# One load for wq, and K and V exchanging their regions of the on-chip buffer, in a decode attention kernel

## The chip, the cores and the metric

The kernel runs on one core of one Trainium2 chip. The metric is device time in microseconds (us) of one execution; lower is better. The engines named below are PE (matrix products), DVE (vector), ACT (scalar) and SP, which does no arithmetic here and only issues the loads. Each core has 16 DMA engines; a load over 128 partitions is cut into packets that all 16 engines carry.

Differences are taken only between kernels of the same batch on the same chip.

## The reference, cut to what matters

One token goes through a gated mix of two branches. Branch A is attention with 32 query heads over 4 groups of cached keys and values; branch B is a small gated MLP.

```python
q = x @ wq                          # wq: 1024 x 4096, bf16, 8.4 MB
scores = q . k_cache * Dh ** -0.5   # k_cache: 4 groups x 65536 x 128, 67 MB
o = softmax(scores) . v_cache       # v_cache: the same size
a = o @ wo                          # 8.4 MB
b = mlp(x, w_in, w_out)             # 7.3 MB and 3.7 MB
out = g * a + (1 - g) * b           # g = sigmoid(sum(x * gate_w))
```

Everything is read once: 162.0 MB for a result of 1024 numbers.

## The kernel before: the parts that matter

One tile `kv` holds all big operands. It has five regions of 32 KB per partition. `load(src, shape, at)` issues a load from SP into the region `at`, and the scheduler adds the waits for whatever still uses those bytes. Issues stay in program order, so one that waits holds up all issues after it.

```python
NKV = 5
kv = big.tile([P, NKV * CT * P], BF16, name="kv")
def load(src, shape, at): ...                       # nc.sync.dma_start(...)
def load_kv(src, g, j, at, n=1): ...                # n tiles of 32 KB per partition
...
win = load(win_view, (KC, F), 3)                    # 56 KB per partition: regions 3 and 4
wq_t = [load(wq_view[:, i * KH:(i + 1) * KH, :], (KH, HD), 1 - i) for i in range(2)]
...                                                 # z from win, q from wq, weights from q
build_w(0)
for j in range(NT):                                 # first group: four K tiles
    k_tile(0, j, load_kv(A_k_cache, 0, j, (2, 1, 0, 3)[j])[0])
    if j == 1:
        build_w(1)
project(load(B_w_out..., (FC, D), 4), ...)
stats(0)
for g in range(1, G):
    for h in range(2):
        kn = load_kv(A_k_cache, g, 2 * h, 1 - h, 2) # K pair: regions 1,2 then 0,1
        for i in ((0, 1), (1, 0))[h]:
            k_tile(g, 2 * h + i, kn[i])
        ...
        vn = load_kv(A_v_cache, g - 1, 2 * h, 3, 2) # V pair: always regions 3,4
        v_tile(g - 1, 2 * h, vn[0])
        if h == 1:
            stats(g)
        v_tile(g - 1, 2 * h + 1, vn[1])
    head_out(g - 1)
```

A K tile is transposed in place on DVE in four pieces; PE multiplies each. The two K pairs of a group overlap by one region, and the order of the tiles is chosen so that the shared region comes free first.

Of the kernel before, what the change touches and what calls it, by code (L numbers as in the profile page):

```python
# [24 lines left out]
WO_SPLIT = ((16,), (8, 4, 2, 1, 1))  # L25
# [4 lines left out]
def kernel(  # L30
# [19 lines left out]
    HD = A_wq.shape[1]  # L50
# [4 lines left out]
    KC = D // P  # L55
# [3 lines left out]
    NT = S // (P * CT)  # L59
# [20 lines left out]
    def same_weights(ins):  # L80
        held.add(ins.ins.name)
# [79 lines left out]
    def load(src, shape, at):  # L161
        n = 1
        for s in shape:
            n *= s
        v = kv[:, int(at * CT * P):int(at * CT * P) + n]
        if len(shape) == 2:
            v = v.rearrange("p (a b) -> p a b", b=shape[1])
        ins = nc.sync.dma_start(out=v, in_=src)  # L168
        if not first_load:
            first_load.append(ins.ins.name)  # L170
        return v

    def load_kv(src, g, j, at, n=1):
        h, i = divmod(j, 2)
        rows = src[0, g, 2 * h * CT * P:2 * (h + 1) * CT * P, :].rearrange(
            "(p c) d -> p (c d)", c=2 * CT)
        v = load(rows[:, i * CT * DH:(i + n) * CT * DH], (n * CT * DH,), at)
        return [v[:, i * CT * DH:(i + 1) * CT * DH] for i in range(n)]
# [9 lines left out]
    KH = KC // 2  # L188
# [1 line left out]
    win = load(win_view, (KC, F), 3)  # L190
    win_t = [win[:, i * KH:(i + 1) * KH, :] for i in range(2)]
    wq_view = A_wq.rearrange("(p c) n -> p c n", c=KC)
    wq_t = [load(wq_view[:, i * KH:(i + 1) * KH, :], (KH, HD), 1 - i) for i in range(2)]


    row = const.tile([P, P], FP32, name="row")
# [147 lines left out]
    for k in range(NHB):  # L344
# [3 lines left out]
                                                                   j=B, e=2),  # L348
# [20 lines left out]
    def build_w(g):  # L369
        for v in range(VC):  # L370
            nc.vector.tensor_tensor(
                out=wt[g % 2][:, v, :, :, v, :],
                in0=qs[:, g].unsqueeze(2).to_broadcast([P, BP, NB, REP]),
                in1=own_n[:].unsqueeze(1).unsqueeze(3).to_broadcast([P, BP, NB, REP]),
                op=ALU.mult)
# [5 lines left out]
    def k_tile(g, j, kn):  # L381
        kb = kn.bitcast(I32)
        n = CC * DH // 2
        s_ps = pss.tile([P, 2 * HN], FP32, name="s_ps", tag="s")
        for v in range(VC):
            nc.vector.transpose(out=kb[:, v * n:(v + 1) * n], in_=kb[:, v * n:(v + 1) * n])  # L386
            while late:
                nc.vector.reduce_max(**late.pop())  # L388
            kx = kn[:, v * CC * DH:(v + 1) * CC * DH].rearrange(
                "p (c h k e) -> p h e c k", h=2, k=B, e=2)  # L390
            for b in range(BP):
                for k in range(2):
                    ins = nc.tensor.matmul(  # L393
                        s_ps[:, k * HN:(k + 1) * HN],
                        lhsT=wt[g % 2][:, v, b].rearrange("p a v h -> p (a v h)"),
                        rhs=kx[:, b // 2, b % 2, k * CC // 2:(k + 1) * CC // 2, :],
                        start=(v == 0 and b == 0), stop=(v == VC - 1 and b == BP - 1),
                        skip_group_check=True)
                    if k > 0:
                        same_weights(ins)  # L400
        if g not in mxs:
            mxs[g] = wk.tile([P, NT], FP32, name="mx")
        sct[g, j] = scp.tile([P, CC * B], BF16, name="sc")
        nc.scalar.copy(out=sct[g, j][:], in_=s_ps[:])  # L404
        late.append(dict(out=mxs[g][:, j:j + 1], in_=sct[g, j][:], axis=AX.X))

    def stats(g):
        nc.vector.reduce_max(**late.pop())  # L408
        m1 = wk.tile([P, 1], FP32, name="m1")
        nc.vector.reduce_max(out=m1[:], in_=mxs[g][:], axis=AX.X)  # L410
        mt_ps = psm.tile([1, P], FP32, name="mt_ps", tag="m")
        nc.tensor.transpose(mt_ps[:], m1[:], ident_f[:])
        gm = wk.tile([1, REP], FP32, name="gm")
        nc.vector.tensor_reduce(out=gm[:], in_=mt_ps[:].rearrange("p (a h) -> p h a", h=REP),
                                axis=AX.X, op=ALU.max)
        gr = wk.tile([1, P // REP, REP], FP32, name="gr")
        nc.vector.tensor_copy(out=gr[:], in_=gm[:].unsqueeze(1).to_broadcast([1, P // REP, REP]))
        nb_ps = psm.tile([P, 1], FP32, name="nb_ps", tag="m")
        nc.tensor.matmul(nb_ps[:], lhsT=gr[:].rearrange("p a h -> p (a h)"),
                         rhs=ones_f[0:1, 0:1], start=True, stop=True)  # L420
        nb = wk.tile([P, 1], FP32, name="nb")
        nc.vector.tensor_scalar(out=nb[:], in0=nb_ps[:], scalar1=-SCALE, scalar2=None,  # L422
                                op0=ALU.mult)
        lss[g] = wk.tile([P, NT], FP32, name="ls")
        for j in range(NT):
            nc.scalar.activation(out=sct[g, j][:], in_=sct[g, j][:], func=ACT.Exp, scale=SCALE,  # L426
                                 bias=nb[:, 0:1], accum_out=lss[g][:, j:j + 1])
            ptt[g, j] = ptp.tile([P, CC, B], BF16, name="pt")
            nc.vector.transpose(out=ptt[g, j][:].rearrange("p c x -> p (c x)"),  # L429
                                in_=sct[g, j][:])  # L430

    def v_tile(g, j, vt):
        if j == 0:
            o_ps[g] = pso.tile([P, 2, VC * DH], FP32, name="o_ps")
        vx = vt.rearrange("p (v c d) -> p c v d", v=VC, d=DH)
        for u in range(CC // 2):
            hs = slice(u % 2 * P // 2, (u % 2 + 1) * P // 2)
            for e in range(2):
                ins = nc.tensor.matmul(  # L439
                    o_ps[g][hs, e, :],  # L440
                    lhsT=ptt[g, j][:, 2 * u:2 * u + 2, :].rearrange("p c x -> p (c x)"),
                    rhs=vx[:, 2 * u + e], start=(j == 0 and u < 2),
                    stop=(j == NT - 1 and u >= CC // 2 - 2), skip_group_check=True)
                if e > 0:
                    same_weights(ins)
# [28 lines left out]
    def keep_busy(n):  # L474
        ps = pss.tile([P, 2 * HN], FP32, name="busy_ps", tag="s")
        w = wt[G % 2][:].rearrange("p v b t u h -> p (v b t u h)")
        for i in range(n):
            ins = nc.tensor.matmul(ps[:, :HN], lhsT=w[:, :P], rhs=w[:, :HN], start=True,  # L478
                                   stop=True, skip_group_check=True)
            if i > 0:  # L480
                same_weights(ins)
# [4 lines left out]
    def project(w, n, vec, c0, first=False, last=False):  # L486
        for c in range(n):
            for t in range(NB):
                nc.tensor.matmul(  # L489
                    out_ps[t * B:(t + 1) * B, :],  # L490
                    lhsT=vec[:, c0 + c:c0 + c + 1].to_broadcast([P, B]),
                    rhs=w[:, c, t * NO:(t + 1) * NO],
                    start=(first and c == 0), stop=(last and c == n - 1),
                    skip_group_check=True)


    build_w(0)
    for j in range(NT):
        k_tile(0, j, load_kv(A_k_cache, 0, j, (2, 1, 0, 3)[j])[0])
        if j == 1:  # L500
            build_w(1)
    project(load(B_w_out.rearrange("(p c) n -> p c n", c=FC), (FC, D), 4), FC, uT, 0, first=True)
    stats(0)
    for g in range(1, G):
        for h in range(2):
            kn = load_kv(A_k_cache, g, 2 * h, 1 - h, 2)
            for i in ((0, 1), (1, 0))[h]:
                k_tile(g, 2 * h + i, kn[i])
            if h == 0 and g + 1 < G:
                build_w(g + 1)  # L510
            vn = load_kv(A_v_cache, g - 1, 2 * h, 3, 2)
            v_tile(g - 1, 2 * h, vn[0])
            if h == 1:
                stats(g)
            v_tile(g - 1, 2 * h + 1, vn[1])
        head_out(g - 1)
    for j, n, at in ((0, 2, 1), (2, 1, 3), (3, 1, 4)):
        for i, vt in enumerate(load_kv(A_v_cache, G - 1, j, at, n)):
            v_tile(G - 1, j + i, vt)
    keep_busy(4)  # L520
# [3 lines left out]

    wo_view = A_wo.rearrange("(p c) n -> p c n", c=OC)
    c0 = 0
    for at, split in enumerate(WO_SPLIT):
        for n in split:
            t = load(wo_view[:, c0:c0 + n, :], (n, D), at + c0 % (OC // 2) * D / (CT * P))
            project(t, n, oa, c0, last=(c0 + n == OC))  # L530
            keep_busy(WO_BUSY[n])
            c0 += n
# [46 lines left out]
```

## Time and profile before

| | before |
|---|---|
| time, median (5 runs) | 383.12 us |
| span of the profiled run | 381.3 us |
| PE, DVE busy | 61%, 57% |
| load queue, share of the time of 16 DMA engines | 98.7% |
| 65,536-byte packet on one engine (median) | 2.421 us |
| last load complete | 378.36 us |

From the page of the kernel before: the span, the busy shares of the engines, the mean DMA share in 40 slices of the span (9 is 90% or more), and the load queue with its packets, megabytes and share of 16 engines' time.

```profile
span 381.3 us, 2601 instructions
PE 233.9 (61%) x1388; PEld 56.2 (15%) x802; DVE 218.5 (57%) x211; ACT 39.6 (10%) x55; POOL 4.4 (1%) x10
...
DMA  9999999999999999999999999999999999999995
...
DMA packets 4231, 162.17 MB, mean 425 GB/s; under 512 B 504, under 2 KB 508, under 8 KB 892
...
q1 hardware_dynamic: 4180, 162.01, 98.7%
```

The loads fill the time; every slice but the last is at 9. A packet of 65,536 bytes in 2.421 us is 27.1 GB/s on one engine and 433 GB/s on 16. The Trainium skill, "DMA: Bandwidth & Descriptors", Specifications, gives 435 GB/s as the fabric ceiling, and this trace agrees within 0.5%. So the DMA engines are not only busy, they are at their rate.

Part 4 of the same page follows the work that ended last back through what released it.

```profile
DMA 58%; PE 25%; DVE 13%; ACT 2%; issue 1%; SPq 1%; DVEq 0%; ACTq 0%
```

Read alone, this chain says that 38% of the time belongs to PE and DVE. It does so because each load was *issued* after some matmul or transpose freed its region. That does not tell whether the issue came late. For this one needs the queue's own times (columns: start, length, operation, count; several issues are merged, so a length covers the waits between them). Kernel before, issues from SP:

```profile
0.79 0.80 SPq L168 DMA_DIRECT2D kv<-in_A_wq_dram  x2
1.64 42.21 SPq L168 DMA_DIRECT2D kv<-in_A_k_cache_dram  x4
43.90 0.92 SPq L168 DMA_DIRECT2D kv<-in_B_w_out_dram  x1
73.52 0.33 SPq L168 DMA_DIRECT2D kv<-in_A_k_cache_dram  x1
96.88 0.33 SPq L168 DMA_DIRECT2D kv<-in_A_v_cache_dram  x1
119.44 0.33 SPq L168 DMA_DIRECT2D kv<-in_A_k_cache_dram  x1
```

The trace also records every packet. Each engine closes a load with a 4-byte packet of 9 ns, so 16 of these in a row show when the first and the last engine finished that load. I call *lead* the time from the issue of a load to the moment at which the first engine finishes the load in front. The issue at 119.44 us has the V pair in front, which the first engine finishes at 123.95 us: a lead of 4.51 us. In the steady state pairs finish 19.36 us apart without exception from 104.59 to 336.90 us, which is 8 packets of 2.42 us per engine. The last engine keeps the same 19.36 us, 2.3 us behind the first. So no pause for an issue shows there.

### The profile page before, as it was taken

Reading aid. Unit: us, or ns where it says so; the run is one execution under the profiler, and the core shown is the slowest. Engines: PE = TensorE matmul, PEld = TensorE weight load, DVE = VectorE, ACT = ScalarE, POOL = GpSimd, SP = SyncE. Lnnn points to the kernel's source line nnn. Section 1 sums busy time; section 2 is a strip of 40 time slices with the busy share of each in tenths; the row PEclk is TensorE's granted clock in tenths of the full one; section 3 lists DMA queues with packets and bytes.
Section 4 is the critical chain, followed back from the end, with each engine's and each line's share of the span. In section 5 each row is a group of like instructions: output and inputs, shape, how many; then the busy total and the mean of one; then the engine's idle time right before and its main releaser. Section 6 shows DMA issues by size and latency. Waiting matters only on the chain.

```text
span 381.3 us, 2601 instructions
## 1 busy us (share of the span) xinstructions
PE 233.9 (61%) x1388; PEld 56.2 (15%) x802; DVE 218.5 (57%) x211; ACT 39.6 (10%) x55; POOL 4.4 (1%) x10
## 2 busy tenths in 40 slices
PE   0064447976247944796397729871977196849375
PEld 0011001111101210111011101120211011212122
DVE  4133478997597506966977059669960488560040
ACT  1001001110601100114010001050100010500000
POOL 4000000000000000000000000000000000000000
PEclk9995659899859895989688958895989579969799
DMA  9999999999999999999999999999999999999995
GB/s 385 430 440 433 414 424 433 440 478 443 421 399 419 433 442 440 440 440 426 440 435 426 440 440 440 428 441 433 399 426 442 433 440 434 413 425 423 433 415 226
DMA packets 4231, 162.17 MB, mean 425 GB/s; under 512 B 504, under 2 KB 508, under 8 KB 892
## 3 DMA queue, kind: packets, MB, share of 16 engines
q1 hardware_dynamic: 4180, 162.01, 98.7%
q8 instruction: 8, 0.13, 0.1%
q14 instruction: 3, 0.02, 0.0%
q10 hardware_dynamic: 40, 0.01, 0.0%
HBM read 162.01 MB, written 0.00 MB: 425 GB/s over the span
## 4 chain that ended last, share of the span: by engine, by line
DMA 58%; PE 25%; DVE 13%; ACT 2%; issue 1%; SPq 1%; DVEq 0%; ACTq 0%
DMA kv<-in_A_k_cache_dram 42%; PE s_ps L393 21%; DMA kv<-in_A_wo_dram 8%; DVE kv L386 7%; DMA kv<-in_A_v_cache_dram 7%; PE o_ps L439 3%; DVE pt L429 2%; DVE o_sb L453 1%; DVE mx L388 1%; ACT sc L404 1%; ACT sc L426 1%; SPq L168 1%; DVE rowt L449 1%; PE om_ps L459 0%; DVE osum L469 0%
## 5 line engine op out<-in xcount | busy, mean ns | idle before, releaser
L393 PE MATMUL s_ps<-kv,wt 128*128 128x512 bf16 x512 | 141.9, 438 | 81.9 <-DVE kv L386 81.9
L386 DVE STREAM_TRANSPOSE kv<-kv 128x2048 int32<-128x2048 int32 x64 | 142.7, 2280 | 55.9 <-DMA kv<-in_A_k_cache_dram 55.9
L439 PE MATMUL o_ps<-kv,pt 128*64 128x512 bf16 x512 | 61.9, 400 | 7.4 <-DMA kv<-in_A_v_cache_dram 7.4
L393 PEld LDWEIGHTS <-wt 128*128 128x128 bf16 x256 | 27.6, 108 | 197.4 <-issue 138.8
L404 ACT CAST sc<-s_ps 128x1024 bf16<-128x1024 f32 x16 | 16.2, 1012 | 249.9 <-PE s_ps L393 249.9
L439 PEld LDWEIGHTS <-pt 128*64 128x64 bf16 x256 | 16.1, 115 | 50.6 <-issue 48.1
L429 DVE STREAM_TRANSPOSE pt<-sc 128x1024 bf16<-128x1024 bf16 x16 | 18.6, 1217 | 6.8 <-ACT sc L426 6.8
L388 DVE TENSOR_REDUCE mx<-sc 128x1 f32<-128x1024 bf16 x12 | 14.5, 1209 | 10.1 <-ACT sc L404 10.1
L426 ACT ACTIVATE sc<-sc,nb 128x1024 bf16<-128x1024 bf16 x16 | 18.2, 1136 | 12.2 <-DVE nb L422 12.2
L449 DVE TENSOR_TENSOR rowt<-o_ps,own 128x1024 f32<-128x1024 f32 x4 | 4.8, 1195 | 24.9 <-PE o_ps L439 24.9
L459 PE MATMUL om_ps<-o_sb,hsel 128*32 128x128 f32 x8 | 2.3, 388 | 18.7 <-DVE o_sb L453 18.7
L408 DVE TENSOR_REDUCE mx<-sc 128x1 f32<-128x1024 bf16 x4 | 4.9, 1220 | 13.6 <-ACT sc L404 13.6
L279 PE MATMUL q_ps<-kv,xT 128*32 128x512 bf16 x64 | 7.2, 630 | 4.0 <-DMA kv<-in_A_wq_dram 4.0
L235 PE MATMUL xb_ps<-xg,spread 8*128 8x256 bf16 x1 | 0.4, 367 | 13.4 <-DMA xg<-in_gate_w_dram 13.4
L453 DVE TENSOR_REDUCE o_sb<-rowt 128x128 f32<-128x1024 f32 x4 | 7.5, 1872 | 0.1
L346 DVE TENSOR_TENSOR rowt<-q_ps,own_b 128x512 f32<-128x512 f32 x2 | 1.3, 686 | 9.0 <-PE q_ps L279 9.0
L489 PE MATMUL out_ps<-kv,oa 128*32 128x256 bf16 x128 | 4.6, 274 | 2.7 <-DMA kv<-in_A_wo_dram 2.2
L279 PE MATMUL z_ps<-kv,xT 128*32 128x448 bf16 x64 | 6.0, 568 | 0.0
L239 DVE TENSOR_TENSOR xm<-xb_ps,sel_i 128x128 f32<-128x128 f32 x2 | 0.5, 286 | 8.2 <-PE xb_ps L235 8.2
L535 ACT CAST out_sb<-out_ps 128x256 bf16<-128x256 f32 x1 | 0.4, 372 | 45.1 <-PE out_ps L489 45.1
L478 PE MATMUL busy_ps<-wt 128*128 128x512 bf16 x16 | 4.5, 383 | 0.0
L279 PEld LDWEIGHTS <-xT 128*32 128x32 bf16 x64 | 2.7, 141 | 12.2 <-issue 12.2
(90 smaller groups left out, 59.4 us busy)
## 6 DMA issues: line engine op xcount, KB each, us to landing
kv<-in_A_k_cache_dram SPq DMA_DIRECT2D x4, 4096.0 KB, 48.7
kv<-in_A_wq_dram SPq DMA_DIRECT2D x2, 4096.0 KB, 33.5
kv<-in_A_v_cache_dram SPq DMA_DIRECT2D x2, 4096.0 KB
kv<-in_B_w_in_dram SPq DMA_DIRECT2D x1, 7168.0 KB
kv<-in_A_wo_dram SPq DMA_DIRECT2D x1, 4096.0 KB
kv<-in_B_w_out_dram SPq DMA_DIRECT2D x1, 3584.0 KB
kv<-in_A_wo_dram SPq DMA_DIRECT2D x1, 2048.0 KB
kv<-in_A_wo_dram SPq DMA_DIRECT2D x1, 1024.0 KB, 30.6
```

The source lines that it names most:

```text
L279: ins = nc.tensor.matmul(ps[t * B:(t + 1) * B, k * HN:k * HN + n], lhsT=xT[:, i * KH + c:i * KH + c + 1].to_broadcast([P, B]), rhs=w[:, c, ...
L386: nc.vector.transpose(out=kb[:, v * n:(v + 1) * n], in_=kb[:, v * n:(v + 1) * n])
L388: nc.vector.reduce_max(**late.pop())
L393: ins = nc.tensor.matmul(s_ps[:, k * HN:(k + 1) * HN], lhsT=wt[g % 2][:, v, b].rearrange("p a v h -> p (a v h)"), rhs=kx[:, b // 2, b % 2, ...
L404: nc.scalar.copy(out=sct[g, j][:], in_=s_ps[:])
L408: nc.vector.reduce_max(**late.pop())
L426: nc.scalar.activation(out=sct[g, j][:], in_=sct[g, j][:], func=ACT.Exp, scale=SCALE, bias=nb[:, 0:1], accum_out=lss[g][:, j:j + 1])
L429: nc.vector.transpose(out=ptt[g, j][:].rearrange("p c x -> p (c x)"), in_=sct[g, j][:])
L439: ins = nc.tensor.matmul(o_ps[g][hs, e, :], lhsT=ptt[g, j][:, 2 * u:2 * u + 2, :].rearrange("p c x -> p (c x)"), rhs=vx[:, 2 * u + e], sta ...
L449: nc.vector.tensor_tensor(out=om8, in0=o_ps[g][:].rearrange("p e (v d) -> p (e v) d", d=DH), in1=own_8[:].unsqueeze(2).to_broadcast([P, 2 ...
L453: nc.vector.tensor_reduce(out=o_sb[:], in_=om8.rearrange("p x d -> p d x"), axis=AX.X, op=ALU.add)
L489: nc.tensor.matmul(out_ps[t * B:(t + 1) * B, :], lhsT=vec[:, c0 + c:c0 + c + 1].to_broadcast([P, B]), rhs=w[:, c, t * NO:(t + 1) * NO], st ...
```

## The change

Its intent: wq needs two neighbouring regions to come as one load of 64 KB per partition. With K in the low regions, as before, K tile 1 would then have to wait for all of wq. So K moves to the three high regions, where w_in comes free early, and V to the two low ones. The order of tiles in a K pair is mirrored with it, and the last V tiles and wo are placed anew.

```diff
-    wq_t = [load(wq_view[:, i * KH:(i + 1) * KH, :], (KH, HD), 1 - i) for i in range(2)]
+    wq = load(wq_view, (KC, HD), 0)
+    wq_t = [wq[:, i * KH:(i + 1) * KH, :] for i in range(2)]
 ...
-    for j in range(NT):
-        k_tile(0, j, load_kv(A_k_cache, 0, j, (2, 1, 0, 3)[j])[0])
+    for j, n, at in ((0, 1, 2), (1, 1, 3), (2, 1, 0), (3, 1, 1)):
+        for i, kn in enumerate(load_kv(A_k_cache, 0, j, at, n)):
+            k_tile(0, j + i, kn)
 ...
-            kn = load_kv(A_k_cache, g, 2 * h, 1 - h, 2)
-            for i in ((0, 1), (1, 0))[h]:
+            kn = load_kv(A_k_cache, g, 2 * h, 2 + h, 2)
+            for i in ((1, 0), (0, 1))[h]:
 ...
-            vn = load_kv(A_v_cache, g - 1, 2 * h, 3, 2)
+            vn = load_kv(A_v_cache, g - 1, 2 * h, 0, 2)
 ...
-    for j, n, at in ((0, 2, 1), (2, 1, 3), (3, 1, 4)):
+    for j, n, at in ((0, 2, 2), (2, 1, 1), (3, 1, 0)):
 ...
-    for at, split in enumerate(WO_SPLIT):
+    for at, split in zip((4, 2), WO_SPLIT):
```

## The prediction

> **What bounds the kernel now.** The loads. The page's queue part gives the load queue 98.7% of the span of all 16 DMA engines, for 162.0 MB. In the trace's packet records a 65,536-byte packet takes a median of 2.421 us: 433 GB/s on 16 engines. The Trainium skill, "DMA: Bandwidth & Descriptors", Specifications, gives 435 GB/s as the fabric ceiling; this trace agrees within 0.5%. Packets start at 1.0 us, the last load lands at 378.4 us, and between I find no pause: from 104.6 to 336.9 us the first engines finish a K or V pair every 19.36 us. Outside the stream lie 1 us at the start and 2.9 us at the end (last projection, copy, store). The chain of waits alternates K load, transposes, matmuls and a load's issue, but an issue only has to come before the queue runs dry: from 119 us on it comes 3.6 to 5.4 us before the first engine finishes the load in front. PE (61% busy) and DVE (57%) have slack.
>
> **What the change removes, adds, moves.**
> - wq: each engine gets 8 packets of 64 KB instead of 16 of 32 KB: 2.421 against 2 x 1.213 us. Estimate: 0 to 0.1 us gained; the two halves together took the 19.36 us of a 64 KB pair. One issue (0.4 us) goes, off the path.
> - The first half of q's matmuls no longer runs at 31.8 us (3.61 us) but after the whole wq landed (38.9 us). q's matmuls end near 46.6 instead of 43.0 us, the weight build near 51.1 instead of 47.5 us, so the first K tile starts 0.8 us after its landing at 50.3. Before, DVE waited 0.84 us for the second K tile at 59.3 us: that swallows the delay.
> - K tile 1 may load once w_in is used (near 26.5 instead of 35.5 us). K tiles 2 and 3 and w_out wait for all of wq: issued near 46.7 us, with K tiles 0 and 1 queued until 57 us. No bubble.
> - The first V pair no longer waits for w_out's projection: 2.5 us earlier than 96.9 us, invisible behind a full queue.
> - Steady state: a mirror image, with the same waits.
> - Tail: the last head's V tile 2 goes where the later of two V tiles comes free, so it is issued at 332.8 instead of 328.0 us. The load in front finishes at 336.9 us: 4.1 us of lead, like the others.
>
> **On the critical path:** almost nothing of it. Same bytes, no new bubble, same instruction order on PE and DVE.
>
> **Predicted:** 383.1 us, 8 in 10 between 382.6 and 383.7. Faster by over 2%: 0.5%; within: 98%; slower: 1.5%.
>
> **What would show it.** 256 packets of 32,768 bytes become 128 of 65,536. PE idles once before q's matmuls, until near 39 us, and they take 7.2 us. Second K load issued near 26.5 us, two K loads and w_out near 46.7 us. First K transposes near 51 us, second K tile at 60 us. First V issue near 94.5 us. Load share 98 to 99%, pairs 19.36 us apart, last landing at 378.3 us.
>
> **What would make it wrong.** A tile freed later than I read, above all a lower granted clock at 325 to 333 us (1.0 now) that slows the V tile before the last issues past 335 us: 1 to 3 us lost. Instruction fetches (eight 16 KB packets) that hit other DMA engines: each sets one engine back some 1.5 us, and the slowest ends the stream: up to 1.5 us either way.

## More of the kernel before

A batch repeats the kernel before; it took 383.12, 383.07, 383.23 and 383.13 us (medians) in the four batches of this study. The changed kernel was timed in the first batch only, so the experiments that are built on it are compared with the kernel before as well.

## The result, and the profile after

| | before | after |
|---|---|---|
| median | 383.12 us | 382.93 us |
| all runs | 383.06 to 383.21 | 382.74 to 383.05 |
| ratio, 95% interval | | 0.9995, 0.9981 to 1.0008 |

A ratio here is the ratio of the fast runs, and it is not quite the ratio of the medians. The interval holds 1: the time is the same within the noise. The page of the changed kernel:

```profile
span 381.1 us, 2600 instructions
PE 230.3 (60%) x1388; PEld 55.6 (15%) x802; DVE 218.4 (57%) x211; ACT 39.6 (10%) x55; POOL 4.4 (1%) x10
...
DMA  9999999999999999999999999999999999999995
...
DMA packets 4087, 162.17 MB, mean 426 GB/s; under 512 B 488, under 2 KB 492, under 8 KB 876
...
q1 hardware_dynamic: 4036, 162.01, 98.7%
...
DMA 49%; PE 26%; DVE 19%; ACT 3%; issue 2%; SPq 1%; DVEq 0%; ACTq 0%
```

There are 144 packets fewer: 128 data packets (256 of 32 KB became 128 of 64 KB) and the 16 closing packets of one load. The load queue's share is the same. The last line is part 4 of the page: the chain has moved nine points from DMA to DVE and others, in a run of the same length. So the shares of that chain were not shares of a bound here.

The issues of the changed kernel:

```profile
0.78 0.33 SPq L168 DMA_DIRECT2D kv<-in_A_wq_dram  x1
1.16 44.04 SPq L168 DMA_DIRECT2D kv<-in_A_k_cache_dram  x4
45.25 0.44 SPq L168 DMA_DIRECT2D kv<-in_B_w_out_dram  x1
73.44 0.33 SPq L168 DMA_DIRECT2D kv<-in_A_k_cache_dram  x1
95.74 0.33 SPq L168 DMA_DIRECT2D kv<-in_A_v_cache_dram  x1
119.36 0.33 SPq L168 DMA_DIRECT2D kv<-in_A_k_cache_dram  x1
```

Taken singly, the four K issues stand at 1.64, 35.48, 43.05 and 43.42 us before, and at 1.16, 23.79, 42.58 and 44.87 us after. K tile 1 is issued 11.7 us earlier and nothing comes of it, because the queue has work until 47 us anyway.

The matmuls of q, by the view of the tile `q_ps` (shortest, median and longest duration in ns, first and last start in us), before and then after:

```profile
L279 PE MATMUL q_ps<-kv,xT x64: 585/634/635, 31.8 to 42.4; 128*32 128x512 bf16 x64
```

```profile
L280 PE MATMUL q_ps<-kv,xT x64: 379/631/634, 38.9 to 44.4; 128*32 128x512 bf16 x64
```

Before they ran in two bursts of 3.61 us with a wait between; after, in one of 5.90 us. The shortest one of the single burst takes 379 ns and not 585. The granted clock tells why; here are busy times by stretch in the changed kernel (PE busy and count first; clock, DMA share and GB/s last):

```profile
35.00:40.00 5.00, 1.08 (x12) 0.30 (x7) 0.00 (x0) 0.00 (x0) 0.00 (x0) 0.50 0.97 419
40.00:45.00 5.00, 4.82 (x56) 1.06 (x25) 0.12 (x1) 0.00 (x0) 0.00 (x0) 0.65 0.97 416
```

The burst starts at the granted 0.50, and the mean of the next stretch is 0.65. The Trainium skill, "TensorE: Matmul & The Clock Gate", Part 1, states that a cold PE runs at half clock and is released after about 3.4 us of sustained work. This trace agrees in kind: the granted clock stays at 0.50 until 4.6 us after the burst's start and is 1.00 for its end, while each of the two bursts of 3.61 us before was over at 0.50. The delay itself is not fixed: it was 3.1 us in run e9 and 5.8 us in run e1, both described below.

DVE after q, first before, then after (start, length, operation, count; in brackets the idle time in front and what ended it):

```profile
46.63 0.89 DVE L371 TENSOR_TENSOR wt<-qs,own_n 128x128 bf16<-128x128 bf16 x4
50.36 8.89 DVE L386 STREAM_TRANSPOSE kv<-kv 128x2048 int32<-128x2048 int32 x4 [2.84 <-DMA kv<-in_A_k_cache_dram]
60.09 2.31 DVE L386 STREAM_TRANSPOSE kv<-kv 128x2048 int32<-128x2048 int32 x1 [0.84 <-DMA kv<-in_A_k_cache_dram]
```

```profile
48.51 0.89 DVE L372 TENSOR_TENSOR wt<-qs,own_n 128x128 bf16<-128x128 bf16 x4
49.92 8.89 DVE L387 STREAM_TRANSPOSE kv<-kv 128x2048 int32<-128x2048 int32 x4 [0.53 <-DMA kv<-in_A_k_cache_dram]
59.72 2.31 DVE L387 STREAM_TRANSPOSE kv<-kv 128x2048 int32<-128x2048 int32 x1 [0.91 <-DMA kv<-in_A_k_cache_dram]
```

The weights are ready 1.9 us later, and DVE still waits 0.53 us for the first K tile and 0.91 us for the second. The later q was paid out of idle time alone.

### The profile page after: what moved, and what is told of

The parts are those of the page before. It is cut to its first block, busy times and chain, and to the rows that moved or that the text cites. A ratio compares the mean times of both kernels' runs of the same rounds, so it can differ in the third digit from the quotient of the medians.

```text
span 381.1 us, 2600 instructions
## 1 busy us (share of the span) xinstructions
PE 230.3 (60%) x1388; PEld 55.6 (15%) x802; DVE 218.4 (57%) x211; ACT 39.6 (10%) x55; POOL 4.4 (1%) x10
## 3 DMA queue, kind: packets, MB, share of 16 engines
q1 hardware_dynamic: 4036, 162.01, 98.7%
## 4 chain that ended last, share of the span: by engine, by line
DMA 49%; PE 26%; DVE 19%; ACT 3%; issue 2%; SPq 1%; DVEq 0%; ACTq 0%
DMA kv<-in_A_k_cache_dram 33%; PE s_ps L394 21%; DVE kv L387 11%; DMA kv<-in_A_wo_dram 8%; DMA kv<-in_A_v_cache_dram 7%; DVE pt L430 4%; PE o_ps L440 3%; DVE mx L389 2%; ACT sc L405 2%; DVE o_sb L454 1%; ACT sc L427 1%; DVE rowt L450 1%; SPq L168 1%; PE om_ps L460 0%; ACT L427 0%
## 5 line engine op out<-in xcount | busy, mean ns | idle before, releaser
L280 PE MATMUL q_ps<-kv,xT 128*32 128x512 bf16 x64 | 5.9, 548 | 8.8 <-DMA kv<-in_A_wq_dram 8.8
L280 PE MATMUL z_ps<-kv,xT 128*32 128x448 bf16 x64 | 4.5, 455 | 0.0
```

The lines of the kernel that those rows point to most:

```text
L280: ins = nc.tensor.matmul(ps[t * B:(t + 1) * B, k * HN:k * HN + n], lhsT=xT[:, i * KH + c:i * KH + c + 1].to_broadcast([P, B]), rhs=w[:, c, ...
```

## The experiments

Two theories stood at the start. **A**: the queue of loads never runs empty, so only its bytes count, and the change moves work inside slack. **B**: the chain of waits is the bound; parts of the change help and other parts hurt, and they cancel. Twelve kernels were run, in three batches.

**e1: the single wq load alone.** In the kernel before:

```diff
-    wq_t = [load(wq_view[:, i * KH:(i + 1) * KH, :], (KH, HD), 1 - i) for i in range(2)]
+    wq = load(wq_view, (KC, HD), 0)
+    wq_t = [wq[:, i * KH:(i + 1) * KH, :] for i in range(2)]
```

> The kernel before with only the single 64 KB wq load (regions as before). Theory A (the load queue is never empty, so only its bytes and its slowest engine count): same as before, 383.1 us within 0.3; the second K load is issued near 43 us instead of 35.5 us and nothing comes of it. If the 0.19 us of the whole change come from one issue or 128 packets fewer, this run shows them alone: 382.9 us. Rival B (parts of the change help and hurt and cancel): this part without the freed K region loses, 1 to 4 us (383.9 to 387 us), since q's first half of 3.6 us is no longer hidden.

383.51 us (382.86 to 383.77), ratio 1.0010, interval 0.9997 to 1.0022: no difference that is clear of noise, but not the clean 383.1 either. K tile 1 was issued at 45.34 us, 2.28 us before the first engine ran out; that load was done 0.2 us late in the trace, its first packets taking up to 1.9 us against 1.21. Rival B's 383.9 to 387 us did not come. Whether those tenths come from that issue was the question for e9.

**e2: wq in two loads, new regions kept.** In the changed kernel:

```diff
-    wq = load(wq_view, (KC, HD), 0)
-    wq_t = [wq[:, i * KH:(i + 1) * KH, :] for i in range(2)]
+    wq_t = [load(wq_view[:, i * KH:(i + 1) * KH, :], (KH, HD), i) for i in range(2)]
```

> The changed kernel with wq in two loads again, new regions kept. Theory A: 383.1 us within 0.3, with 256 packets of 32 KB in place of 128 of 64 KB. Rival B: this keeps the good part (regions) and drops the bad one (late q), so 1 to 4 us faster than before, 379 to 382 us.

383.05 us, ratio 1.0002 (0.9988 to 1.0015). The size of wq's packets is worth nothing that can be measured, and the new regions hold no hidden gain.

**e3: the end undone.** In the changed kernel:

```diff
-    for j, n, at in ((0, 2, 2), (2, 1, 1), (3, 1, 0)):
+    for j, n, at in ((0, 2, 2), (2, 1, 0), (3, 1, 1)):
```

> The changed kernel, but the last head's V tile 2 goes to region 0 and tile 3 to region 1, so tile 2 is issued near 327.5 us again and not at 332.2 us. Theory A: the load in front finishes on its first engine at 336.9 us, so both issue times come early enough: 382.9 us within 0.3. Rival B: the late issue costs something at the end, so 0.5 to 2 us faster (381 to 382.4 us).

383.06 us, ratio 1.0001 (0.9988 to 1.0013). V tile 2 was issued at 328.19 us again instead of 332.19 us; a lead of 4.7 us was enough.

**e4: a quarter of the K transposes taken away** (wrong result). In the changed kernel:

```diff
         for v in range(VC):
-            nc.vector.transpose(out=kb[:, v * n:(v + 1) * n], in_=kb[:, v * n:(v + 1) * n])
+            if v < VC - 1:
+                nc.vector.transpose(out=kb[:, v * n:(v + 1) * n], in_=kb[:, v * n:(v + 1) * n])
```

> Wrong result on purpose: one of the four transposes of every K tile is left out, 16 x 2.28 = 36.5 us of VectorE work. Theory A: VectorE is not the bound, 382.9 us within 0.4. Rival B (the printed chain of waits is the bound; 11% of it is these transposes): a quarter of 11% of 381 us, 10 us, comes off: 373 us.

382.95 us, ratio 0.9997 (0.9983 to 1.0010). From its page, the busy shares and part 4:

```profile
PE 230.3 (60%) x1388; PEld 55.9 (15%) x802; DVE 183.5 (48%) x195; ACT 39.6 (10%) x55; POOL 4.4 (1%) x10
...
DMA 58%; PE 25%; DVE 13%; ACT 2%; issue 1%; SPq 1%; DVEq 0%; ACTq 0%
```

DVE lost 34.9 us of work and the time did not move: theory B fails for DVE's part of the chain. The chain line is, word for word, that of the kernel before, whose DVE had all its work. (The comparison with the reference did not flag this run, nor the next one; they are wrong by construction all the same.)

**e5: half of wq loaded** (wrong result), all other loads and all compute kept:

```diff
-    wq = load(wq_view, (KC, HD), 0)
-    wq_t = [wq[:, i * KH:(i + 1) * KH, :] for i in range(2)]
+    wq = load(wq_view[:, :KH, :], (KH, HD), 0)
+    wq_t = [wq, wq]
```

> Wrong result on purpose: only half of wq is loaded (used twice), 4.19 MB less, all other loads and all compute kept. Theory A: 8 packets of 32 KB fewer per engine at 1.213 us is 9.7 us less: 373.2 us within 0.5. Rival B (chain of waits): wq is ahead of that chain by its K landings only in part; less than half of that, 378 us or more.

373.37 us against 383.23, ratio 0.9745 (0.9731 to 0.9760). From its page:

```profile
span 371.4 us, 2600 instructions
...
q1 hardware_dynamic: 4036, 157.81, 98.7%
```

That is 9.86 us less for 4.19 MB less; 8 packets of 1.213 us are 9.70 us. Bytes count at the full rate of the engines, while 34.9 us of DVE work in e4 counted nothing. This run also speaks for PE, whose work no run took away: PE had all its work here, and the kernel still became faster by the time of the bytes.

**e6, e7, e8: delays, to find how much slack there is.** In the changed kernel, with `r` = 1, 2, 3 idle reductions after the first transpose of each of the six K pairs:

```diff
+    lag = const.tile([P, DH], FP32, name="lag")
 ...
             nc.vector.transpose(out=kb[:, v * n:(v + 1) * n], in_=kb[:, v * n:(v + 1) * n])
+            if v == 0 and g > 0 and j in (1, 2):
+                for _ in range(r):
+                    nc.vector.tensor_reduce(out=lag[:], in_=om8.rearrange("p x d -> p d x"),
+                                            axis=AX.X, op=ALU.add)
```

> In each of the six K pairs of heads 1 to 3, one idle VectorE reduction (1.87 us, result unused) after the first transpose of the pair, so that every later issue of a load comes 1.9 us later after its K landing. 11.2 us of work on the printed chain in all. Theory A: the shortest lead of an issue over the end of the load in front falls from 3.5 to about 1.6 us, still enough if a load needs about 1 us from issue to first packet: 382.9 us within 0.4. Rival B: up to 6 x 1.87 = 11 us slower, 394 us.

385.80 us (384.69 to 385.98), ratio 1.0062 (1.0047 to 1.0077). My number was wrong: the delay did cost 2.6 us. The profiled run, at 384.69 us the fastest of the four, shows where. Three loads of pairs with leads of 1.95, 1.62 and 1.84 us finished 0.47, 0.65 and 0.49 us late on their first engine; pairs with leads of 2.6 us and more finished within 0.08 us of their time. The one with the shortest lead was issued here:

```profile
200.20 0.33 SPq L168 DMA_DIRECT2D kv<-in_A_k_cache_dram  x1
```

> The same with two reductions (3.74 us) per K pair. Theory A: the shortest leads fall to about -0.2 us and the longest to 1.6 us, so some loads start 0.5 to 1.5 us late: 384 to 392 us, with pauses between landings of pairs (more than 19.36 us apart) exactly where the lead is under about 1 us. Rival B: up to 22 us slower, 405 us.

397.01 us (395.73 to 399.77), ratio 1.0371 (1.0329 to 1.0412); above the range I gave. In its trace three pairs were issued 0.57 to 2.56 us after the first engine had run out, and each finished 1.5 to 1.6 us later than that delay alone explains. My "exactly where the lead is under about 1 us" was wrong too: a pair with a lead of 2.00 us finished 0.43 us late, another with 2.01 us only 0.05 us late.

> The same with three reductions (5.61 us) per K pair. Theory A: every lead of these loads is used up; each further 1.87 us of delay now costs about its own length per K pair, so about 6 x 1.9 = 11 us more than the run with two reductions: 395 to 405 us. Rival B: in proportion to the run with one, three times its loss (416 us).

405.31 us (403.70 to 406.40), ratio 1.0587 (1.0569 to 1.0605). The median is 0.3 us above the range, and 8.3 us more than e7 where I had expected about 11. Here the first engine runs dry before an issue six times. From its page, and a stretch around one of the two longest pauses, the other being at 296 us (DMA share and GB/s are the last two numbers):

```profile
DMA  9999999999998999799949999999959998989995
...
q1 hardware_dynamic: 4036, 162.01, 94.6%
```

```profile
205.00:213.00 8.00, 7.31 (x29) 1.44 (x14) 6.27 (x5) 1.01 (x1) 0.00 (x0) 0.87 0.40 133
```

The load issued at 210.61 us came 3.85 us after the first engine had finished the one in front. Its first packets started 0.96 to 1.51 us after the issue, and most of them then took 3.1 us instead of 2.42. In this run each load issued after the queue was empty finished about 1.6 us later than its issue delay alone explains. I had expected "about 1 us", which is only the first of these two parts.

**e9 and e10: a late q, without and with the exchange of regions.** Eight idle matmuls between the halves of q; e9 in kernel e1, e10 in the changed kernel:

```diff
         x_rows(q_ps, wq_t[i], HN, i)
+        if i == 0:
+            lag_ps = pss.tile([P, 2 * HN], FP32, name="lag_ps", tag="s")
+            w0 = wt[0][:].rearrange("p v b t u h -> p (v b t u h)")
+            for _ in range(8):
+                nc.tensor.matmul(lag_ps[:, :HN], lhsT=w0[:, :P], rhs=w0[:, :HN], start=True,
+                                 stop=True, skip_group_check=True)
```

> The kernel before with one wq load (as in e1) and eight idle matmuls (128x512, result unused) between the two halves of q's matmuls, some 2 to 3.5 us, so that wq's space comes free that much later. There K tile 1 waits for that space. From e1 (issue at 45.3 us, load in front ends at 47.6 us on its first engine): the issue comes at about 48 us, after the queue has run dry, so a pause of about 2 to 3 us: 385 to 386.5 us. If a late wq does not matter to the queue: 383.2 us.

383.09 us (383.03 to 383.17), ratio 0.9998 (0.9983 to 1.0013): a miss, as the dose that I wanted did not come about. The issue came at 46.16 us, only 0.8 us later than in e1, because the second half of q ran in 1.91 us, where the kernel before took 3.61 us; the granted clock from 40 to 45 us was 0.79 in e9, 0.54 in e1 and 0.68 in the kernel before. Still the lead was 1.34 us, shorter than e1's 2.28 us. The first engine finished K tile 1 late by 0.13 us, but the slowest engine, which lay 1.77 us behind the first, by nothing (49.27 to 58.99 us, 9.72 us as is usual for such a load). So a late issue of this size need not cost anything. In e1's trace it did: with the slowest engine 1.84 us behind the first, about the same distance, that load took 9.95 us on the slowest engine, 0.23 us more than is usual. Why the longer lead of e1 cost more than the shorter one of e9 stays open, and so the late issue is not shown to be the cause of e1's 0.4 us.

> The changed kernel with the same eight idle matmuls. K tile 1 was issued near 24 us into a region that wq does not hold; only K tiles 2 and 3 and w_out wait for wq, with the queue filled until 57 us. So 383.0 us within 0.3 although q and the first K tile come 2 to 3.5 us later. If q is on the path: 385 us or more.

383.05 us (382.90 to 383.18), ratio 0.9996 (0.9982 to 1.0011). K tile 1 was issued at 23.75 us; the later issues had leads of 14.7 us and more. As expected, q's lateness costs nothing there, but since it cost nothing in e9 either, this pair does not show that the exchange of regions protects from anything at this dose.

**e11: one wq load, K tile 1 moved to region 3 without the exchange.** In kernel e1:

```diff
-        k_tile(0, j, load_kv(A_k_cache, 0, j, (2, 1, 0, 3)[j])[0])
+        k_tile(0, j, load_kv(A_k_cache, 0, j, (2, 3, 1, 0)[j])[0])
```

> The kernel before with one wq load and K tile 1 of the first head in region 3 (free early), K tile 2 in 1, tile 3 in 0; V stays high and K low. Then no early issue is late, but the first K pair of the second head (regions 1 and 2) has to wait for K tile 2, near 84 us instead of 73 us, while the load in front (w_out) ends at 85.3 us on its first engine: a lead of 1 to 1.5 us. e6 lost 0.5 to 0.65 us at leads of 1.6 to 1.95 us, so 0.5 to 1.5 us here: 383.5 to 384.6 us. If a lead of 1 us were enough: 383.1 us.

384.18 us (383.21 to 384.74), ratio 1.0023 (1.0006 to 1.0041). The first K pair was issued at 84.56 us, with a lead of 0.61 us, and finished 0.91 us late on the first engine and 0.84 us late on the slowest. This is a real loss, though a small one: it is what a placement that looks as good can cost when its region comes free 11 us later.

**e12: half the delay of e6.** In the changed kernel, the reduction over half the columns (0.98 us each):

```diff
+            if v == 0 and g > 0 and j in (1, 2):
+                nc.vector.tensor_reduce(out=lag[:, :DH // 2],
+                                        in_=om8[:, :, :DH // 2].rearrange("p x d -> p d x"),
+                                        axis=AX.X, op=ALU.add)
```

> The changed kernel with half a reduction (about 0.95 us) per K pair. The shortest lead falls from 3.5 to about 2.55 us, above the 2.3 us at which the earlier runs began to lose time: 383.0 us within 0.3. If each delay on the printed chain counts: 388 us.

382.94 us (382.89 to 383.03), ratio 0.9994 (0.9977 to 1.0011). The shortest lead was 2.38 us, and that pair finished 19.36 us after the one in front. It was issued here:

```profile
198.92 0.33 SPq L168 DMA_DIRECT2D kv<-in_A_k_cache_dram  x1
```

With e6 this brackets the need where the queue had not run dry before: in e12 a lead of 2.38 us lost nothing, in e6 leads of 1.95 us and less lost 0.47 to 0.65 us. It is not a fixed threshold. In e8, where the queue had just run dry, pairs with leads of 1.63 and 1.65 us finished only 0.07 and 0.04 us late; in e7 one with 2.38 us finished 0.18 us late; and e1's 2.28 us, with packets of 32 KB, went with 0.2 us.

No run with a right result beat both kernels by more than the noise, and none points to a version that would: what is left outside the stream is about 1 us at the start and 2.9 us at the end, and no experiment here tried those.

## Why the prediction was right

- **The bound.** Predicted: the loads, at the engines' rate, without a pause. Right. e5 (bytes taken away and all compute kept, 9.86 us gained) and e4 (DVE work taken away, nothing gained) show it, and pairs finish 19.36 us apart in both kernels.
- **wq.** Predicted: 0 to 0.1 us. e2 finds nothing above noise. wq took 19.36 us on the first engine before (18.50 to 37.86 us) and 19.33 us after (18.61 to 37.94 us).
- **Late q.** The mechanism was right and its size off. q's matmuls took 5.90 us and not 7.2 us, because I carried the low clock of two short bursts over to one long burst, whose last 1.3 us ran at the full clock; they ended near 44.8 us, not 46.6 us. The first K transposes started at 49.92 us (predicted 51), right at their load's landing, so the 0.8 us to be swallowed never arose.
- **Issue times.** Second K load 23.8 us (predicted 26.5), the next two 42.6 and 44.9 us (46.7), first V pair 95.7 us (94.5). The second K load did not have to wait for all of w_in, as I had written: its region 3 holds the first 32 of w_in's 56 KB, and about 20 of the 64 matmuls of z were still to run when it was issued. All with leads of 8.8 us or more, so none mattered.
- **Tail.** Predicted: V tile 2 issued at 332.8 us, lead 4.1 us, harmless. Measured 332.19 us and 4.74 us; e3 shows it harmless.
- **The risks named.** A slower clock at 325 to 333 us did not come (1.00 granted between 320 and 335 us in both traces). The other, instruction fetches, is visible and small: the last load completes at 378.36 us before and 378.17 us after, and the difference is that of the slowest engine's delay behind the first (2.29 against 2.09 us on the big loads near the end). Those 0.19 us equal the difference of the medians. The ratio's interval holds 1, and e2 and e3, each close to the changed kernel, had ratios of 1.0002 and 1.0001, so I do not count the 0.19 us as a gain of the change.
- **What I had not predicted and got wrong on the way:** how much lead is enough. I assumed 1 us in e6 to e8. By e6 and e12 the need of a queue that has not run dry lies between 1.95 and 2.38 us, so the shortest leads of the two kernels, 3.56 and 3.52 us, hold 1.1 to 1.6 us of slack and not 2.5. Within the prediction this did no harm, as every lead it relied on was above 3.5 us.

Open: e1's 0.4 us, which its interval does not separate from zero; and what sets the lead that is needed, for instance whether it is the packet under way, as equal leads cost differently in e6, e7 and e8. No run varied the packet size on purpose for this.

## What to carry to other kernels

When the load queue holds 98 to 99% of the DMA engines' time at their full rate, compare for each load the time of its issue with the time at which the load in front ends, and ignore the shares of the chain of waits. A change that only moved issues and compute inside those leads was not seen here; fewer bytes were, at the engines' rate (9.86 us for 9.70 us of packets). Before spending slack, measure how much is needed by adding idle work in growing doses until the time moves.

## What the Trainium skill lacked or had wrong

- "DMA: Bandwidth & Descriptors", sections "Specifications" and "Latency and other measured facts", gives a first-byte latency of about 0.6 us for loads issued from SP, without saying from which moment. After an empty queue, e8 shows the engines' first packets 0.96 to 1.51 us after the start of the issue at 210.61 us (0.63 to 1.18 us after its end, as it takes 0.33 us), and most of these packets took 3.1 us instead of 2.42. A restart cost about 1.6 us in all. The page has no figure for how early a load must be issued so that a busy queue loses nothing: here 2.38 us was enough in e12 and 1.95 us was not in e6, but the lead alone did not decide it.
- "Runtime: NRT & Kernel Launch", Instruction fetch mechanics, says that instructions are refilled in 16 KiB blocks over a DMA queue of their own, and calls the cost mostly hidden. The traces agree on the blocks (eight packets of 16,384 bytes in the span). But they run on the same DMA engines as the data: at one of them (97.3 us before) one engine fell from 0.01 to 1.56 us behind the first, the fetch taking 1.02 us and the data packet beside it 0.55 us more than usual. Such a set-back can stay: before, the slowest engine's delay behind the first grew from 1.06 to 2.29 us over the load during which the fetch of 43.4 us fell, and was still 2.29 us on the big loads near the end. The page gives no cost of a fetch to a kernel bound by loads.
- "Perfetto Trace Analysis", Identifying the Most-Contended Engine, advises to use HBM utilization for DMA instead of occupancy, which 16 engines make misleading. The queue's busy share over all 16 engines (98.7%, and 94.6% when e8 starved it) together with the packet duration did tell the bound.
- None of the pages says that a chain of last releasers can change its shares by nine points at equal time (DMA 58% before, 49% after), or be the same with 34.9 us of DVE work less (e4).
